# A state-space mixer block: two kernels' filters loaded by channel and turned on TensorE, with step one and the modulation loads reordered

## The chip, the core and the metric

The kernel runs on one core of a Trainium2 chip. The core has a matrix engine (TensorE, in the profile PE, with its weight loads as PEld), three elementwise engines (VectorE or DVE, ScalarE or ACT, GpSimd or POOL), a queue engine that only issues transfers (SyncE or SP), and 16 DMA engines that move data between the chip's memory and the on-chip memory SBUF. TensorE writes its results to PSUM, of which this kernel uses four tiles of 128 x 1024 numbers. Each engine works through its own list of instructions in order; semaphores hold an instruction until what it needs has been done on another engine. The metric is the device time of one execution in microseconds (us).

## The reference

All tensors are float32; S = 2048 tokens, D = 640 channels, F = 1728. Cut to what matters:

```python
mod = (silu(c) @ w_mod).reshape(1, 6, 1, -1);  sa, ca, ga, sb, cb, gb = mod[:, 0], ..., mod[:, 5]
h  = layernorm(x) * (1 + ca) + sa                     # x is A_q
k_shift[t] = sum_s A_k[t - s] * shift_k[:, s]         # causal, 4 taps, per channel
kv = k_shift * A_v
y  = irfft(rfft(kv, 2S) * rfft(ssm_k, 2S))[:S] + kv * ssm_D     # long causal convolution, per channel
x  = x + ga * (h * y)
h  = layernorm(x) * (1 + cb) + sb
x  = x + gb * (gelu(h^T w1 + b1) w2 + b2)^T           # a two-layer network over the token axis
```

The term `kv * ssm_D` is the same as adding `ssm_D` to the first tap of the filter `ssm_k`, and the kernel does that.

## The kernel before, in words

The convolution part goes over five chunks (`c` = 0 to 4) of 128 channels, each in two halves of 64; the network over the tokens follows. A token's number is written as 32 n1 + n2. A partition of SBUF then holds one (half, n1) and, along its free axis, the 32 values of n2 for 64 channels. The transform is done in four small matrix products:

- `step1(side, t)`: step one, over n1. `step1(0, t)` takes kv, which lies in tile X; `step1(1, t)` takes the filter, which lies in tile P under the name KSP. Four calls (t = 0 to 3) make one side. Each is 16 products of a 128 x 64 stationary piece with a 128 x 128 table F1; ScalarE then copies the PSUM tile to Z. KSP's pieces are contiguous, X's have a stride of 32 numbers.
- `f2(g)`, g = 0 to 7: step two, over n2, for both sides, by two tables W2. ScalarE copies the filter's half of the PSUM tile to KT (L249), VectorE multiplies it with kv's half (two products to P, "p<-pst,kt"), and GpSimd adds and subtracts these to the spectrum Y ("y<-p", two a group). P has two buffers for it, so P is both the filter's tile and the products'.
- `i2(r)`, twice: first inverse step, Y to T2. `i1(half)`, twice: second inverse step, by the table V1. `gate` multiplies the result with A1 on VectorE and adds it to x on GpSimd.

PSUM tiles are taken in turn from a ring of three; a fourth, `tap`, holds the taps and the short convolution's sums, and in chunk 0 the modulation's sums.

`kv_ops(g)` is the short convolution of a quarter of a chunk: seven elementwise steps and a product with v that writes a quarter of X. Quarter 2 runs on GpSimd, the others on VectorE. For chunk c + 1 these steps are the list `fill`, from which `dv(n)` takes some between the groups of f2.

The filter of a chunk comes by `load_ks`: two transfers of 64 x 64 pieces of 32 numbers, already in the (half, n1) layout, into KSR (half of the tile `aux`), with `ssm_D` for one partition of each half. `perm_add` adds `ssm_D`, and `perm` on ScalarE (L175) reorders the whole to KSP.

Chunk 0 carries one-time work. `lay_w2(i, n)` on ScalarE (L109) spreads W2 from `xb`, where x's second half will lie. `load_q` brings q (32 transfers, L514) and four of five row blocks of `w_mod` (L346); the fifth goes to P. 16 pairs of `bn_stats` with a `bn_aggr` each (L560, L561), then `rstd`, give the layer norm's scale. `mod_part` (L353) multiplies w_mod's blocks with silu(c), `mod_sum` copies the sums (L357), `mod_row` (L364, copies L371 and L373) spreads three rows over all partitions. `ac` (L300, 16 steps on ScalarE) normalises x into A1, and `po` on VectorE scales and shifts A1 by the modulation, in chunk 0 by halves. w_mod's blocks lie in the tile of V1, and in `aux`, where KSR and A1 also lie; so V1's table (L578) is loaded after `mod_part(1)`, the filter of chunk 1 after `mod_part(2)`.

The order of all of it is written by hand in the program; there is no planner. Transfers carry one of eight semaphores in turn, and each waits on its semaphore's earlier transfer, so the SP queue can stand behind slow transfers. In the list of chunk 0 after f2, the order on TensorE is: four `step1(0, t)` of chunk 1, the transpose of the biases, `i2(0)`, `mod_part` 0 to 3, `i2(1)`, `mod_part` 4, `mod_row`, `i1(0)`, `i1(1)`, four `step1(1, t)`. On ScalarE it is: copies of step one, copies of `i2(0)`, the root, `ac[0:4]`, copies of `i2(1)`, `mod_sum`, `ac[4:8]`, `mod_row`'s copies, `perm(1)`, `ac[8:16]`, copies of step one.

## Time and profile before

| | us |
|---|---|
| median of three runs | 705.45 (703.06 to 716.54) |
| the profiled execution | 705.09 |
| its span in the profile | 703.0 |
| TensorE busy, all matrix products | 643.0 |
| VectorE busy | 494.3 |
| ScalarE busy | 307.9 |
| GpSimd busy | 155.7 |
| first matrix product begins | 23.65 |
| chunk 0's step two (f2) begins | 42.35 |
| chunk 1's step two begins | 113.41 |
| chunk 2's step two begins | 164.86 |
| chunk 3's step two begins | 214.76 |

The span is the time from the first to the last instruction; 2.1 us of the device time lie around it. From one f2 to the next take 71.06 us in chunk 0, where the one-time work lies, and 51.45 and 49.90 us in chunks 1 and 2. A row of the timeline has a start, a length, the engine and line, what is written and read, the shape and the count, and in brackets how long the engine was idle before and what released it. "SPq" and "ACTq" rows are the issuing of transfers, not the transfers themselves.

### The profile page before, as it was taken

To read this page: it belongs to the slowest core of one execution; us is meant where nothing else is said; L and a number is where in the kernel's file an instruction comes from. 1 tells how busy PE (TensorE), PEld (TensorE's weight loads), DVE (VectorE), ACT (ScalarE), POOL (GpSimd) and SP (SyncE) were. 2 spreads that over 40 slices of the span, in tenths; PEclk is the share of its full clock that TensorE was granted. 3 is DMA by queue.
4 is the path that set the end of the run, shared out by engine and by line. 5 is a ranking of instruction groups with operands and counts; after the bars stand their busy time and mean duration, and the time that the engine had idled before them with its cause. 6 is when DMAs were issued, how large, how long until landed. Compare 5 with 4: busy or idle time off the path is not lost.

```text
span 703.0 us, 20726 instructions
## 1 busy us (share of the span) xinstructions
PE 643.0 (91%) x9099; PEld 623.8 (89%) x9099; DVE 494.3 (70%) x865; ACT 307.9 (44%) x477; POOL 155.7 (22%) x135
## 2 busy tenths in 40 slices
PE   0699868989999999987899999999999999999997
PEld 0699558989999999777899999999999999999997
DVE  6678568969879837888895411421398969888886
ACT  0564653635645645645766422422334222333331
POOL 5297038714725527300000000000000000000000
PEclk9999978999999999989889999999999999999999
DMA  9977968527142523352113650353173343555511
GB/s 182 212 221 230 350 135 180 116 48 173 40 86 73 177 54 88 115 133 49 34 28 63 118 104 17 61 115 66 53 195 106 105 137 100 160 171 171 154 55 38
DMA packets 166672, 82.80 MB, mean 118 GB/s; under 512 B 89235, under 2 KB 157622, under 8 KB 166582
## 3 DMA queue, kind: packets, MB, share of 16 engines
q1 hardware_dynamic: 162034, 80.17, 46.2%
q10 hardware_dynamic: 4548, 1.31, 1.1%
q8 instruction: 71, 1.16, 0.7%
q14 instruction: 19, 0.16, 0.1%
HBM read 70.97 MB, written 10.49 MB: 116 GB/s over the span
## 4 chain that ended last, share of the span: by engine, by line
PE 69%; DVE 14%; DMA 6%; POOL 4%; ACT 3%; issue 3%; SPq 1%; ACTq 0%; DVEq 0%; POOLq 0%
PE pst L445 20%; PE pst L1033 18%; PE pst L229 8%; PE pst L1110 7%; PE pst L245 6%; PE pst L274 4%; POOL y L60 4%; PE pst L930 3%; DVE tap L60 2%; DMA aux<-in_A_ssm_k_dram 2%; PE pst L293 2%; DVE kt L60 2%; DMA aux<-in_w_mod_dram 2%; DVE aux L60 2%; DVE p L60 1%
## 5 line engine op out<-in xcount | busy, mean ns | idle before, releaser
L245 PEld LDWEIGHTS pst<-z,w 128*64 128x64 f32 x2560 | 94.7, 141 | 7.7 <-ACT z L231 7.3
L245 PE MATMUL pst<-z,w 128*64 128x64 f32 x2560 | 95.7, 240 | 6.3 <-ACT z L231 6.1
L60 POOL TENSOR_TENSOR y<-p 128x256 f32<-128x256 f32 x72 | 91.9, 1324 | 25.7 <-DVE p L60 25.2
L60 DVE TENSOR_TENSOR p<-pst,kt 128x512 f32<-128x512 f32 x80 | 52.3, 690 | 23.8 <-ACT kt L249 16.1
L229 PE MATMUL pst<-v,x 128*64 128x128 f32 x640 | 45.5, 302 | 23.6 <-DVE x L60 23.6
L231 ACT ACTIVATE z<-pst 128x1024 f32<-128x1024 f32 x40 | 45.6, 1144 | 46.2 <-PE pst L229 26.6
L229 PEld LDWEIGHTS pst<-v,x 128*64 128x64 f32 x640 | 43.6, 221 | 24.1 <-POOL t L470 23.6
L249 ACT ACTIVATE kt<-pst 128x512 f32<-128x512 f32 x40 | 25.2, 631 | 48.0 <-PE pst L245 26.3
L229 PE MATMUL pst<-v,p 128*64 128x128 f32 x640 | 39.9, 285 | 6.5 <-DVE aux L60 5.0
L229 PEld LDWEIGHTS pst<-v,p 128*64 128x64 f32 x640 | 37.4, 144 | 7.8 <-DVE aux L60 5.2
L274 PEld LDWEIGHTS pst<-v,y 32*128 32x128 f32 x1280 | 38.2, 187 | 5.4 <-POOL y L60 2.4
L274 PE MATMUL pst<-v,y 32*128 32x64 f32 x1280 | 40.1, 272 | 2.4 <-DVE y L60 1.4
L1033 PE MATMUL pst<-r_z,m_w 128*128 128x320 f32 x222 | 41.6, 309 | 0.7 <-DVE m_w L60 0.7
L1021 ACT ACTIVATE m_w<-m_v 128x896 fp32r<-128x896 f32 x24 | 22.2, 948 | 38.8 <-DVE m_v L60 23.1
L60 DVE TENSOR_TENSOR tap<-tap,kt 128x512 f32<-128x512 f32 x51 | 35.6, 698 | 1.3
L60 DVE TENSOR_TENSOR kt<-in,tap 128x512 f32<-128x512 f32 x51 | 35.1, 688 | 1.5
L1033 PEld LDWEIGHTS pst<-r_z,m_w 128*128 128x128 f32 x222 | 34.8, 188 | 0.9 <-DVE m_w L60 0.9
L850 ACT ACTIVATE pst<-pst,sm 128x640 f32<-128x640 f32 x14 | 10.7, 766 | 56.0 <-PE pst L445 56.0
L60 DVE TENSOR_TENSOR m_w<-m_v,m_w 128x896 fp32r<-128x896 f32 x24 | 26.0, 1088 | 9.8 <-ACT m_w L1021 9.8
L282 ACT ACTIVATE z<-pst 128x512 f32<-128x512 f32 x38 | 21.5, 666 | 21.1 <-PE pst L274 21.1
L1021 ACT ACTIVATE m_w<-m_p 128x896 fp32r<-128x896 f32 x12 | 11.4, 954 | 41.2 <-DVE m_p L60 24.4
L293 PEld LDWEIGHTS pst<-z,v 64*64 64x64 f32 x1280 | 22.4, 144 | 7.6 <-issue 4.9
(304 smaller groups left out, 1449.5 us busy)
## 6 DMA issues: line engine op xcount, KB each, us to landing
x<-in_B_w_dram SPq DMA_DIRECT2D x20, 512.0 KB
m_v<-in_B_w_dram SPq DMA_DIRECT2D x15, 384.0 KB
x<-in_B_w_dram SPq DMA_DIRECT2D x14, 384.0 KB
aux<-in_A_ssm_k_dram SPq DMA_DIRECT2D x10, 512.0 KB
in<-in_A_k_dram SPq DMA_DIRECT2D x36, 128.0 KB
in<-in_A_v_dram SPq DMA_DIRECT2D x36, 128.0 KB
m_x<-xs SPq DMA_DIRECT2D x28, 160.0 KB
out_dram<-m_x SPq DMA_DIRECT2D x28, 160.0 KB
```

Of the source, the lines that this page charges most:

```text
L60: TT = lambda eng, o, a, b, op: eng.tensor_tensor(o, a, b, op=op)
L229: pe.matmul(ps[64 * ri:64 * ri + 64, o:o + 128], lhs, F1[:, 128 * ri:128 * ri + 128], start=True, stop=True)
L231: evac = lambda: act.activation(Z[:, side, t].rearrange("p a k e -> p e a k"), ps.rearrange("p (e a k) -> p e a k", a=8, e=2), AF.Copy)
L245: pe.matmul(ps[64 * h:64 * h + 64, o:o + 64], W2[k1 // 32][:, 2 * (k1 % 32) + ri], rhs, start=True, stop=True)
L249: act.activation(kt.rearrange("p (m i) -> p m i", i=32), pv[:, :, 1], AF.Copy)
L274: pe.matmul(pp[qd // 2][:, o:o + 64], Y[p, ri, i:i + 2].rearrange("p i k -> p (i k)"), V2[p, 64 * ri:64 * ri + 64], start=ri == 0, stop=ri ...
L282: act.activation(o, i, AF.Copy)
L293: pe.matmul(ps[64 * b:64 * b + 64, 512 * e + 64 * jj:512 * e + 64 * jj + 64], V1[p, ri, n2], T2[p, :, 32 * ri + n2], start=ri == 0, stop=r ...
L445: pe.matmul(ps[0:m, h, 0:320], w_.bitcast(F32R), r_[:, 320 * h:320 * h + 320].bitcast(F32R), start=first and i == 0, stop=last and i == 2)
L1021: act.activation(W[n][0].bitcast(F32R), A[p, w_], AF.Copy)
L1033: pe.matmul(bank[n], w[:, i].bitcast(F32R), r.bitcast(F32R), start=i == 0 and k == 0, stop=i == 6 and k == 2)
L1110: pe.matmul(acc[s][:, h, 0:320], w[:, f_].bitcast(F32R), u[r + h].bitcast(F32R), start=f_ == 0 and k == 0, stop=f_ == NF - 1 and k == 2)
```

## The change

Five edits, all in the work of the first two chunks.

1. The filters of chunks 0 and 1 are loaded by channel: `load_kc` is one transfer with a channel's 2048 taps per partition (128 x 2 x 4096 bytes), and `ssm_D` goes to one number per partition. A 128 x 128 identity, EYE, is loaded beside the small constants.
2. `turn` takes the place of `perm_add` and `perm` for these two chunks. It adds `ssm_D` to one column (ScalarE in chunk 0, GpSimd in chunk 1), makes 64 products of a 128 x 64 stationary piece (stride 32 numbers) with 64 columns of EYE, in two PSUM tiles, and copies each to KSP on ScalarE.
3. In chunk 0 the filter's step one comes ahead of kv's. `lay_w2(0, ...)` stays with kv's step one. The short convolution's quarter 1 of chunk 1 moves from before f2 to `fill`, which now has 16 steps instead of 8.
4. `load_q` is cut in four: eight transfers of q, then one block of w_mod, four times. The first two parts are issued ahead of kv's step one, the last two after `lay_w2(1, 3)` as before.
5. Chunk 0 after f2: the transpose of the biases and the silu move into f2 (at g = 5); `mod_part` 0 to 3 come ahead of `i2(0)`; `ac[0:8]` ahead of the copies of `i2(1)`; `ac[8:16]` and all of `po` ahead of `turn(1)`; GpSimd's quarter 2 of chunk 2 after `turn(1)`'s addition, and all of it ahead of `i1`.

```diff
+    def load_kc(c, eng=sync):
+        sync.dma_start(KSR, dram(ssm_k, DC * c * S, [[S, 128], [1, S]]), max_dma_last_dim=4096)
+        eng.dma_start(dcol[:, c:c + 1], dram(ssm_D, DC * c, [[1, 128], [1, 1]]))
+
+    def turn(c, eng=act):
+        r, d = KSR[:, 0:1], dcol[:, c:c + 1]
+        if eng is act:
+            act.activation(r, r, AF.Identity, bias=d)
+        else:
+            TT(eng, r, r, d, ALU.add)
+        for s in range(2):
+            ps = psum()
+            for n in range(16):
+                for h in range(2):
+                    pe.matmul(ps[64 * h:64 * h + 64, 64 * n:64 * n + 64],
+                              KSR.rearrange("p (a n) -> p n a", n=32)[:, 16 * s + n], EYE[:, 64 * h:64 * h + 64],
+                              start=True, stop=True)
+            act.activation(KSP.rearrange("p i (n e) -> p n e i", e=2)[:, 16 * s:16 * s + 16],
+                           ps.rearrange("p (n e i) -> p n e i", n=16, e=2), AF.Copy)
...
     sync.dma_start(SM, dram(c_small, 0, [[550, 128], [1, 422]]))
-    load_ks(0, act)
+    sync.dma_start(EYE, dram(c_small, 422, [[550, 128], [1, 128]]))
+    load_kc(0, act)
...
-    perm_add(0)
-    perm(0)
+    turn(0)
+    for t in range(4):
+        step1(1, t)
     all_taps()
     load_taps(2)
...
+    load_q(0, 4, 0)
+    load_q(4, 8, 1)
+    lay_w2(0, 0)
     for t in range(4):
         step1(0, t)
-        lay_w2(0, t)
+        if t < 3:
+            lay_w2(0, t + 1)
     run(kv_ops(2, pool))
     run(kv_ops(0))
-    run(kv_ops(1))
-    for t in range(4):
-        step1(1, t)
...
-    fill = kv_ops(3)
+    fill = kv_ops(1) + kv_ops(3)
...
                 if g == 3:
-                    load_q()
+                    load_q(8, 12, 2)
+                    load_q(12, 16, 3)
+            if c == 0 and g == 5:
+                ps = psum()
+                pe.transpose(ps[:, 0:36], stg, ID[0:36, 0:36])
+                act.activation(cols, ps[:, 0:36], AF.Copy)
+                act.activation(sil, cols[:, 30:35], AF.Silu)
...
             for t in range(4):
                 step1(0, t)
-            ps = psum()
-            pe.transpose(ps[:, 0:36], stg, ID[0:36, 0:36])
-            act.activation(cols, ps[:, 0:36], AF.Copy)
-            act.activation(sil, cols[:, 30:35], AF.Silu)
-            i2(0)
             for kk in range(4):
                 mod_part(tap, kk, pl[kk])
...
                 if kk == 2:
-                    load_ks(1)
+                    load_kc(1)
+            i2(0)
             rstd(rs1, nm1, 0, 16)
-            run(ac[0:4])
-            i2(1)
+            run(ac[0:8])
             mod_part(tap, 4, pl[4])
...
+            i2(1)
             mod_sum(tap, T_kt[:, 0:640])
-            run(ac[4:8])
             pool.tensor_scalar(PW, TR.rearrange("p (i s) -> p s i", s=4), 1.0, None, op0=ALU.mult)
-            run(kv_ops(2, pool))
             for i in range(3):
                 mod_row(i, T_kt[:, 0:640])
+            run(ac[8:16])
+            run(po)
+            turn(1, pool)
+            run(kv_ops(2, pool))
             taps()
             load_taps(3)
-            perm_add(1, dve)
-            perm(1)
             load_ks(2)
-            run(ac[8:16])
-            run(po[0:2])
```

More of the change, by code (lines that the diff above doesn't have):

```diff
@@ L42, in _constants @@
     v1 = np.tile(np.stack([np.cos(ang), np.sin(ang)], 1).reshape(64, 4096) / 2048, (2, 1))
-    sel = np.zeros((128, 128))
-    sel[0, 0:64] = sel[1, 64:128] = 1
-    small = np.concatenate([f1.reshape(128, 256), v2, np.eye(128)[:, 0:36], np.tile(np.eye(2), (64, 1)), sel], 1)
+    small = np.concatenate([f1.reshape(128, 256), v2, np.eye(128)[:, 0:36], np.tile(np.eye(2), (64, 1)),
+                            np.eye(128)], 1)
     return {"small": small.astype(np.float32), "w2": w2.reshape(128, 4096).astype(np.float32),
@@ L132, in mixer_kernel @@
     epsc = small(1)
+    dcol = small(2)
     B1C, B2C = cols[:, 0:14], cols[:, 14:30]
@@ L659, in mixer_kernel @@
                 k0 = step1(1, 0, True)
-            elif half:
-                run(po[2:4])
             gate(c, ps, half)
```

17 lines of the change are left out of this document (8 added, 9 removed).

## The prediction, made before the changed kernel ran

> **What bounds the kernel now.** I read the page's chain of waits first, then the same chain in order of time. Only chunks 0 and 1 are changed, so only the chain up to chunk 1's step two matters. Columns: start, length, what the chain goes through.
>
> ```profile
> 1.94 3.96 DMA in<-in_A_k_dram
> ...
> 42.35 19.09 PE pst L245 x505
> ...
> 65.82 10.93 DMA aux<-in_w_mod_dram
> ...
> 78.82 15.99 DMA aux<-in_A_ssm_k_dram
> ...
> 106.11 6.13 PE pst L229 x64
> ...
> 112.26 1.10 ACT z L231
> ...
> 113.41 2.61 PE pst L245 x63
> ```
>
> TensorE sets the end, except where a load does. There are two such places: 23.65 us before the first product, and the stretch from the end of f2 to 113.41, where the chain runs through w_mod (10.93) and then through chunk 1's filter (15.99). While that filter is late, ScalarE's list stands at `perm`, with `ac[8:16]`, `po` and the gates queued behind. I call T0 the start of chunk 0's f2 (42.35) and T1 that of chunk 1's (113.41); T1 - T0 is 71.06. All the change can do is move T0 and T1 - T0. After T1 nothing is altered, and I count it at nothing: chunk 2's filter is asked for earlier, not later.
>
> **T0.** The early part, first all engines, then TensorE alone, then ScalarE alone:
>
> ```profile
> 9.95 0.36 SPq L465 DMA_DIRECT2D v<-in_const_small_dram  x1
> ...
> 11.22 5.05 SPq L163 DMA_DIRECT2D aux<-in_A_ssm_k_dram  x2
> ...
> 21.27 1.28 ACT L175 ACT_TABLE_LOAD   x1 [21.27 <-DMA aux<-in_A_ssm_k_dram]
> ...
> 40.21 11.04 SPq L514 DMA_DIRECT2D xa<-in_A_q_dram  x16
> ```
>
> ```profile
> 23.65 10.52 PE L229 MATMUL pst<-v,x 128*64 128x128 f32 x128 [23.65 <-DVE x L60]
> 33.98 7.17 PE L229 MATMUL pst<-v,p 128*64 128x128 f32 x128
> 42.35 19.00 PE L245 MATMUL pst<-z,w 128*64 128x64 f32 x511 [1.20 <-ACT z L231]
> ...
> 61.25 8.24 PE L229 MATMUL pst<-v,x 128*64 128x128 f32 x127
> ```
>
> ```profile
> 33.26 1.15 ACT L109 ACTIVATE w<-xb,v 128x1024 f32<-128x1024 f32 x1
> 34.30 1.16 ACT L231 ACTIVATE z<-pst 128x1024 f32<-128x1024 f32 x1
> ```
>
> And TensorE by stage (busy time, records, granted clock as noted, DMA share, GB/s):
>
> ```profile
> 24.00:27.00 3.00, 3.00 (x32) 1.00 1.29 191
> 36.00:39.00 3.00, 3.00 (x60) 1.00 0.93 338
> 80.00:83.00 3.00, 3.00 (x98) 1.00 1.02 410
> ```
>
> The old filter was there at 21.27, 5.0 after its last issue ended (16.27). In the new order it is third after the small constants, behind EYE; at the 1.27 from 9.95 to 11.22 a place, it is issued at 12.5. A transfer of 128 KB took 3.96 from issue to landing (the chain's first row above); the other 0.9 MB at the rate of the 4096-byte rows of V1's table (410 GB/s in the last stage) adds 2.2. So it lands at 18.7; bounds 16.6 (1 MB alone after 1.5) and 21.3 (as before).
>
> A profile record is half a product here: step one has 16 products and 32 records. `turn` has 64 products, so 128 records. No row has its shape. Its stationary piece is X's (128 x 64, stride of 32 numbers), with half the streamed columns. X's step one takes 8.24 / 128 = 64 ns a record, KSP's contiguous one 7.17 / 128 = 56; f2, with 64 columns and contiguous pieces, 19.0 / 511 = 37. If streaming is the limit, `turn` takes 128 x 37 = 4.8; if the strided weight load is, 8.2; at the mean of X's first, slow pass (10.52 / 128 = 82) 10.5. I take 8.2: with equal streaming only the stride can explain X's 64 against KSP's 56.
>
> The sum: landed 18.7, addition on ScalarE 0.3 (an estimate), turn 8.2, last copy 1.15 (as L231's, of equal size), the filter's step one 7.2, kv's 8.2, last copy 1.15: 44.9, which is 2.5 later than 42.35. What is gained is the wait to 23.65 and the slow start that X's pass paid: 32 records in 3 us at first, 60 later (the clock column says 1.00 there only because nothing is on record so early). Now `turn` stands in that slow time. ScalarE doesn't add: a `lay_w2` and a copy start 1.04 apart, 2.08 a group against step one's 2.06.
>
> The Trainium skill ("TensorE: Matmul & The Clock Gate", section LDWEIGHTS) has a weight load take its column count / 1.2 ns whatever the pattern: 53 ns for 64 columns, so 6.8 us a turn and 2.8 less in the end. The trace doesn't settle it: X's 64 ns speaks for more, f2's 37 for less.
>
> **f2 with sixteen fill steps instead of eight.** VectorE in f2 before:
>
> ```profile
> 45.62 1.29 DVE L60 TENSOR_TENSOR p<-pst,kt 128x512 f32<-128x512 f32 x2 [3.45 <-ACT kt L249]
> 46.84 0.68 DVE L60 TENSOR_TENSOR tap<-tap,kt 128x512 f32<-128x512 f32 x1
> 47.55 0.72 DVE L60 TENSOR_TENSOR kt<-in,tap 128x512 f32<-128x512 f32 x1
> 48.16 1.28 DVE L60 TENSOR_TENSOR p<-pst,kt 128x512 f32<-128x512 f32 x2
> ...
> 63.42 0.88 DVE L560 BATCH_NORM_STATS2 sm<-xa 128x6 f32<-128x320 f32 x2
> ```
>
> GpSimd's additions in f2, as a group (count, busy time, mean ns):
>
> ```profile
> L60 POOL TENSOR_TENSOR y<-p 128x256 f32<-128x256 f32 x16 | 20.3, 1329 | 1.2 <-DVE p L60 1.2
> ```
>
> The pair of products takes 1.22 from start to start, a fill step 0.66. The last step of quarter 0 writes X, so now it waits for kv's step one, which ends at T0 - 1.2, and all of quarters 1 and 3 stands behind it on VectorE. Before, X was free at 34.2 (23.65 + 10.52) with the filter's step one still to come, so quarters 0 and 1 were done ahead of f2. From T0: three steps to +1.6, pair 0 at +3.3 (45.62 - 42.35) to +4.5; with 3, 3, 3, 2, 2 steps between, pairs end at 7.8, 11.0, 14.3, 17.0, 19.5. f2(g) needs the PSUM tile of three groups before, and the transpose at g = 5 takes one of the ring, so f2(6) waits for pair 4 (17.0) and f2(7) for pair 5 (19.5). f2 ends at +21.9 instead of 61.25 - 42.35 = +18.9, the last pair at +23.8 instead of +21.1 (63.42). GpSimd, two additions a pair of 1.27 (20.3 / 16), ends at +26.6, hidden by the step one that follows. Cost 3.0 on TensorE, 2.7 on VectorE.
>
> **From f2 to T1.** Durations before:
>
> ```profile
> 70.67 3.79 PE L274 MATMUL pst<-v,y 32*128 32x64 f32 x124 [0.63 <-ACT z L231]
> ...
> 74.31 2.23 ACT L282 ACTIVATE z<-pst 128x512 f32<-128x512 f32 x4 [2.10 <-PE pst L274]
> ...
> 74.38 2.35 PE L353 MATMUL tap<-v,sm 128*32 128x320 f32 x24
> ...
> 76.56 1.28 ACT L337 ACT_TABLE_LOAD   x1
> ...
> 78.13 11.29 SPq L163 DMA_DIRECT2D aux<-in_A_ssm_k_dram  x2
> ...
> 79.59 0.31 ACT L337 ACTIVATE sm<-sm 128x16 f32<-128x16 f32 x1 [1.75 <-DVE sm L561]
> ...
> 81.52 1.65 ACT L300 ACTIVATE aux<-xa,sm 128x128 f32<-128x128 f32 x4 [1.62 <-DVE sm L342]
> ...
> 86.29 0.72 ACT L357 ACTIVATE kt<-tap 96x640 f32<-96x640 f32 x1
> ...
> 87.06 1.37 PE L364 MATMUL pst<-kt,sm 1*128 1x320 f32 x12 [1.61 <-ACT kt L357]
> ...
> 88.44 0.70 ACT L371 ACTIVATE g<-pst 128x640 f32<-128x640 f32 x1
> ...
> 95.19 2.49 DVE L60 TENSOR_TENSOR aux<-aux,g 128x1024 f32<-128x1024 f32 x2
> ...
> 100.47 4.25 DVE L60 TENSOR_TENSOR aux<-aux,g 128x1024 f32<-128x1024 f32 x2 [1.47 <-ACT aux L300]
> ...
> 149.71 2.10 PE L293 MATMUL pst<-z,v 64*64 64x64 f32 x128
> ```
>
> From T0, in the new order: f2 ends 21.9; kv's step one 8.2, 30.1; `mod_part` 0 to 3, 48 records at 2.35 / 24, 4.7, 34.8; `i2(0)` 3.8, 38.6; its copies 2.2 on ScalarE, 40.8; the root's table 1.3, 42.1. The 16 statistics, 63.42 to 79.59 and so 16.1, end at 39.9 and are hidden by 2.2; before they were what the root waited for. Root to first `ac` 1.9 (79.59 to 81.52), 44.0; eight `ac` at 0.41, 47.3; copies of `i2(1)` 2.0, 49.3; `mod_sum` to `mod_row` 0.8 (86.29 to 87.06), 50.1; to the first copy of a row 1.4, 51.5; that copy, which frees `turn`'s PSUM tile, 0.7, 52.2; `turn(1)` 8.2, 60.4; `i1` twice 4.2, 64.6; the filter's step one 4 x 1.85 = 7.4 (the pace of 7.17 with its hand-overs), 72.0; copy 1.1. T1 - T0 = 73.1, against 71.06: 2.0 more.
>
> Beside this path: `ac[8:16]` ends at 56, `po` (a pair of 2.49, and one of 4.25 as where GpSimd worked beside it) by 60.5, so the gates wait for `i1`, not for `po`. w_mod's first four blocks need only be there at T0 + 30: 36 issues of q and w_mod at 0.69 (11.04 / 16) from 36 on (q could start at 40.21 before, and all ahead of it in SP's list comes some 5 sooner) and 10.93 to land end at T0 + 27, so that wait goes. SP is past chunk 1's filter with one issue instead of 11.29 us of it, so k and v of chunk 2 are asked for some 10 us sooner and GpSimd's quarter 2 is done before `po`'s second half. The filter is released by `mod_part(2)` at T0 + 33.6, behind V1's 2 MB: 3 MB at 410 GB/s plus 2 is T0 + 43, 9 before `turn(1)`. Were it later than that, each microsecond over 9 would count in full.
>
> So the 15.99 us wait goes, but the time is taken by what is late next: the modulation's sums, which wait on ScalarE behind the root and eight `ac`, then 8.2 us of products that TensorE didn't have. **Sum: 2.5 + 2.0 = 4.5 on the profiled 705.09 (span 703.0 and 2.1 around it): 709.6.** That execution is 0.4 under the median of the runs shown.
>
> **Rivals.** (a) Streaming sets the pace of the turns: 4.8 us each, the filter at 16.6. That takes off 3.4 twice and 2.1: 700.7. For it: f2's 37 ns at equal columns. Against: X's 64. (b) The identity products don't warm the clock, and the first of the filter's step one runs as the first of kv's did: 10.52 - 8.24 = 2.3, once, at T0: 711.9. The Trainium skill ("TensorE: Matmul & The Clock Gate", Part 4: PE-mode transpose) says that transposes in that mode don't count as busy for the clock. No run here shows it. These are plain products. TensorE also stands still from T0 + 43 to + 50 ahead of `turn(1)`; were both turns at 82 ns, 2.3 each, 714.2. (c) The other side: weight loads of strided pieces no longer hide. Count, busy time and mean ns of X's on the page:
>
> ```profile
> L229 PEld LDWEIGHTS pst<-v,x 128*64 128x64 f32 x640 | 43.6, 221 | 24.1 <-POOL t L470 23.6
> ```
>
> Each takes 221 ns, and they cost 64 only because about three are under way at once. If 64 columns are too short to cover them and each waits for the one before, a turn is 128 x 0.221 = 28.3, 20.1 more twice: 749.8. It decides from about 100 ns a record on (4.8 more a turn), where the kernel is 2% slower. Against it: f2's loads hide behind equally short products. (d) The change doesn't do what it says: the filter's transfer, behind V1, is late again and `turn(1)` waits at T0 + 60 instead of 52: 8 more, 717.6.
>
> **Chances.** Forecast (706 to 713) 0.46; (a) and the stretch from it to 705, 0.25; (b) 0.15; (d) 0.05; (c) or another pile-up beyond 719 0.06; a gain of over 14 us 0.03. A measurement of this kernel tells about 2% (14 us) from no change. The range 700 to 717 takes in the bounds of landing and turn, and leaves out (c), (d) and what lies under (a). Faster by over 2% 0.03, slower 0.07, the rest within.
>
> **What would show it.** The first identity product at 18 to 19 us, 128 records in about 8 us each time, f2 of chunk 0 from 44.9 and lasting 22, no wait of TensorE for w_mod or the filter, the root's table directly ahead of the root with the statistics done before it, chunk 1's f2 at about 118. It is wrong if a turn takes 5 us, or if f2 isn't stretched by VectorE, or if TensorE still waits for a load between f2 and T1.

## The result, and the profile after

The changed kernel takes 712.96 us (median of four runs, 711.82 to 714.70). Beside the kernel before it is 1.011 times as long, with a 95% interval of 1.0072 to 1.0147: slower by 1.1%, less than the 2% that the prediction took for the limit of what can be told apart, and yet clearly told apart. Two of the runs of the kernel before (716.54 and 716.56) were in a slower state, which some executions of any kernel are in, and the ratio leaves them out. The profiled execution took 711.82 us, its span 710.0, against 705.09 and 703.0 before: 7.0 more of span.

TensorE's work in order of time, in the changed kernel, up to the start of chunk 1's f2 (start, length, what, in brackets the idle time before it and what ended it):

```profile
19.29 8.09 PE L194 MATMUL pst<-rows,aux 128*64 128x64 f32 x128 [19.29 <-ACT aux L187]
29.38 8.61 PE L250 MATMUL pst<-v,p 128*64 128x128 f32 x128 [2.00 <-ACT p L197]
37.83 8.16 PE L250 MATMUL pst<-v,x 128*64 128x128 f32 x128
47.53 14.65 PE L266 MATMUL pst<-z,w 128*64 128x64 f32 x384 [1.55 <-ACT z L252]
...
64.62 5.07 PE L266 MATMUL pst<-z,w 128*64 128x64 f32 x128 [2.26 <-DVE p L59]
69.48 8.29 PE L250 MATMUL pst<-v,x 128*64 128x128 f32 x128
...
97.15 2.53 PE L385 MATMUL pst<-kt,sm 1*128 1x320 f32 x12 [4.14 <-ACT kt L378]
100.49 8.13 PE L194 MATMUL pst<-rows,aux 128*64 128x64 f32 x128 [0.81 <-POOL t L59]
108.55 4.17 PE L314 MATMUL pst<-z,v 64*64 64x64 f32 x256
112.65 0.88 PE L250 MATMUL pst<-v,p 128*64 128x128 f32 x12
114.48 6.55 PE L250 MATMUL pst<-v,p 128*64 128x128 f32 x116 [0.95 <-issue]
122.20 3.03 PE L266 MATMUL pst<-z,w 128*64 128x64 f32 x76 [1.17 <-ACT z L252]
```

T0 is 47.53 (before 42.35, so 5.2 later) and T1 122.20 (before 113.41, 8.8 later); T1 - T0 has grown from 71.06 to 74.67. The two waits of TensorE for loads are gone: no row between 69.48 and 122.20 is released by a DMA. In their place stand the turn (8.13), and a wait of 4.14 for the modulation's sums on ScalarE. The chain of waits, in order of time, goes another way through the same stretch (start, length, what it goes through):

```profile
94.74 2.50 POOL t L59 x2
...
100.49 8.13 PE pst L194 x128
```

It leads through GpSimd's work on quarter 2, because that work's fourth step happened to end at 99.92. The turn has no need of it: its addition to the filter stands ahead of it in GpSimd's list, and ended at 93.1. What it waited for is its PSUM tile, freed by the copy of the first modulation row, which starts at 99.69 and takes 0.70. The releaser in a chain is inferred, and has to be held against the list of the program.

The same stretch by windows of TensorE (busy time, records, granted clock, DMA share, GB/s):

```profile
30.00:31.00 1.00, 1.00 (x14) 0.50 0.97 219
...
33.00:34.00 1.00, 1.00 (x22) 1.00 0.96 381
...
95.00:97.00 2.00, 0.00 (x0) 0.50 0.54 124
...
101.50:102.50 1.00, 1.00 (x22) 0.50 0.88 202
...
104.50:106.00 1.50, 1.50 (x29) 1.00 0.00 0
```

A window counts every record that it touches, so that the counts are a little above the pace. Behind chunk 0's turn the clock falls to 0.50 (28.90 to 32.31), and 14 records of step one touch a microsecond instead of 22. It falls once more at 90.34 and is back at 103.99, so the rows ran at half clock: 2.53 instead of 1.37. ScalarE's row of the turn's second copy:

```profile
27.41 1.91 ACT L197 ACTIVATE p<-pst 128x1024 f32<-128x1024 f32 x1 [1.81 <-PE pst L194]
```

It takes 1.91, where L231's of the same 128 x 1024 numbers took 1.16 in the kernel before. After T1 1.8 comes back: chunk 1, from its f2 to chunk 2's, takes 50.26 (122.20 to 172.46) instead of 51.45, and the rest 0.6 less.

### The profile page after: what moved, and what is told of

It is laid out like the page before. It is cut to its first block, busy times and chain, and to the rows that moved or that the text cites. A ratio compares the mean times of both kernels' runs of the same rounds, so it can differ in the third digit from the quotient of the medians.

```text
span 710.0 us, 21234 instructions
## 1 busy us (share of the span) xinstructions
PE 651.9 (92%) x9355; PEld 632.9 (89%) x9355; DVE 494.2 (70%) x863; ACT 312.6 (44%) x480; POOL 153.9 (22%) x134
## 4 chain that ended last, share of the span: by engine, by line
PE 62%; DVE 16%; DMA 6%; POOL 6%; ACT 4%; issue 3%; SPq 3%; ACTq 0%; DVEq 0%; POOLq 0%
PE pst L466 17%; PE pst L1054 17%; PE pst L1131 7%; PE pst L250 5%; PE pst L295 4%; POOL y L59 4%; PE pst L266 4%; PE pst L951 3%; DVE tap L59 2%; DMA in<-in_A_k_dram 2%; PE pst L314 2%; DVE p L59 2%; DVE kt L59 2%; DMA xa<-in_A_q_dram 1%; SPq L143 1%
## 5 line engine op out<-in xcount | busy, mean ns | idle before, releaser
L250 PE MATMUL pst<-v,x 128*64 128x128 f32 x640 | 43.1, 292 | 0.0
L250 PEld LDWEIGHTS pst<-v,x 128*64 128x64 f32 x640 | 41.4, 220 | 0.5
L250 PE MATMUL pst<-v,p 128*64 128x128 f32 x640 | 38.3, 280 | 3.4 <-ACT p L197 2.0
L250 PEld LDWEIGHTS pst<-v,p 128*64 128x64 f32 x640 | 36.4, 141 | 4.1 <-ACT p L197 2.1
L1042 ACT ACTIVATE m_w<-m_v 128x896 fp32r<-128x896 f32 x24 | 22.2, 948 | 38.0 <-DVE m_v L59 23.8
L194 PEld LDWEIGHTS pst<-rows,aux 128*64 128x64 f32 x256 | 16.0, 220 | 21.0 <-ACT aux L187 19.3
L194 PE MATMUL pst<-rows,aux 128*64 128x64 f32 x256 | 16.2, 312 | 20.1 <-ACT aux L187 19.3
```

Source lines behind the costliest of these rows:

```text
L194: pe.matmul(ps[64 * h:64 * h + 64, 64 * n:64 * n + 64], KSR.rearrange("p (a n) -> p n a", n=32)[:, 16 * s + n], EYE[:, 64 * h:64 * h + 64] ...
L250: pe.matmul(ps[64 * ri:64 * ri + 64, o:o + 128], lhs, F1[:, 128 * ri:128 * ri + 128], start=True, stop=True)
L1042: act.activation(W[n][0].bitcast(F32R), A[p, w_], AF.Copy)
```

## The experiments

In what follows, T1 - T0 and the length of a chunk are differences of the starts of f2 in TensorE's rows. Ratios are to the kernel before, with 95% intervals; a single run has none.

**A second profile of both kernels, first, since it says how far one profile can be trusted.** Nothing is edited.

> The changed kernel once more, unaltered, for a second profile. If T0 (47.5), the clock's fall behind the turn and f2's length (22.1, no stop marked issue) belong to the kernel, they are the same within 0.3; if they belong to the execution, T0 is 46.0 as in the kernels with the same head and no fall (46.0 and, with shorter turns, 43.4), or f2 is 24 to 25.

> The kernel before once more, unaltered, for a second profile. If f2 without stops (19.1) belongs to the kernel, it is 19.1 again, and T0 42.3; if stops come with the execution, f2 is 20 to 22 in some executions of it too, and T0 41.0 to 42.4 as in the kernels that share its head.

TensorE's rows of the changed kernel, second execution, and then of the kernel before, second execution:

```profile
29.34 8.87 PE L250 MATMUL pst<-v,p 128*64 128x128 f32 x128 [2.00 <-ACT p L197]
...
47.71 14.48 PE L266 MATMUL pst<-z,w 128*64 128x64 f32 x384 [1.43 <-ACT z L252]
```

```profile
42.04 18.98 PE L245 MATMUL pst<-z,w 128*64 128x64 f32 x511 [1.18 <-ACT z L231]
```

T0 is 47.71 and 42.04, f2 22.2 and 19.0, T1 - T0 74.91 and 71.13: all within 0.3 of the first. The slow step one behind the turn came again. Only some places where the clock falls differ from one execution to the next: in the kernel before 90.56 and 104.21 in the first, 72.69, 89.75 and 106.82 in the second. The differences belong to the kernels, as far as two executions of each can say.

**The head undone.** Chunk 0 as before; chunk 1's turn and w_mod among q's loads stay.

```diff
-    load_kc(0, act)
+    load_ks(0, act)
...
-    turn(0)
-    for t in range(4):
-        step1(1, t)
+    perm_add(0)
+    perm(0)
...
+    run(kv_ops(1))
+    for t in range(4):
+        step1(1, t)
-    fill = kv_ops(1) + kv_ops(3)
+    fill = kv_ops(3)
```

> Chunk 0 as in the kernel before (its filter by partitions and copied, kv's step one first, quarter 1 of kv ahead of f2); chunk 1 by channels and turned, w_mod among q's loads. Theory: the loss lies in chunk 0's head. Then T0 is 42.4 as before (47.53 in the changed kernel), f2 lasts 18.9 (22.1), and the rest of T1 - T0 is as in the changed kernel: T1 - T0 = 74.67 - 3.2 = 71.5, some 8 us off 712: 704, the same as before within 0.5%. Rival: the turn of chunk 1 and its hand-overs cost most of it: then T0 + f2 come back but T1 - T0 stays near 74, and the time is 707 to 709. Second rival: q starts later here (40 instead of 37), so w_mod is late at T0 + 27 and TensorE waits for it, up to 6 us: 705 to 710.

715.49 us, ratio 1.0104 (1.0055 to 1.0152). T0 came back as expected, to 41.46, but T1 - T0 rose to 85.4. TensorE's rows, then its windows:

```profile
80.78 2.36 PE L374 MATMUL tap<-aux,sm 128*32 128x320 f32 x12 [6.82 <-DMA aux<-in_w_mod_dram]
83.07 7.11 PE L295 MATMUL pst<-v,y 32*128 32x64 f32 x128
```

```profile
88.00:90.00 2.00, 2.00 (x44) 0.50 1.25 235
```

The second rival holds in kind: w_mod is late by 6.8. Its total of 705 to 710 is passed all the same, because the clock falls in that wait (at 78.49), so that `i2(0)` takes 7.11 instead of 3.80, and because f2 lasts 20.7. With the old head SP asks for q at 41.72, with the new one at 36.96: w_mod among q's loads is there in time only behind the new head.

**Chunk 1's turn undone.**

```diff
-                    load_kc(1)
+                    load_ks(1)
...
-            turn(1, pool)
+            perm_add(1)
+            perm(1)
```

> The changed kernel with chunk 1's filter loaded by partitions and copied on ScalarE, in the place of the turn. TensorE has 8.1 us less to do between the rows of the modulation and the inverse step. Theory 1: the turn stands on the path with its whole 8.1 us: T1 - T0 falls from 74.7 to about 66.5, 704. Theory 2: the products of VectorE with the modulation's rows (7.4 us, until T0 + 62) and the gates behind them take the turn's place, since the inverse step's two PSUM tiles wait for the gates: T1 - T0 about 70.5, 708. Rival: the filter, 11.3 us of issues behind V1, lands at T0 + 50 or later and TensorE waits for it: T1 - T0 74 or more, 712 and above. T0 stays at 47.5 in all.

711.24 us, ratio 1.0078 (1.0042 to 1.0114). From f2's end to T1 the changed kernel needs 52.5 (69.7 to 122.2) and this one 48.0:

```profile
69.64 1.64 PE L266 MATMUL pst<-z,w 128*64 128x64 f32 x40 [0.96 <-issue]
...
112.66 5.46 PE L250 MATMUL pst<-v,p 128*64 128x128 f32 x96 [1.23 <-DVE aux L59]
119.31 19.57 PE L266 MATMUL pst<-z,w 128*64 128x64 f32 x512 [1.19 <-ACT z L252]
```

Of the turn's 8.1 us 4.5 come back, and VectorE's products and the gates (its `aux`, until 113.7) take the place of the rest: theory 2. T1 - T0 is 73.3 and not its 70.5, because f2 lasted 25.2 here, with stops of 4.3 marked issue. T0 was 46.0 here, not 47.5: with the same pause behind the turn the clock did not fall.

**The copy behind the turn.**

```diff
-            act.activation(KSP.rearrange("p i (n e) -> p n e i", e=2)[:, 16 * s:16 * s + 16],
-                           ps.rearrange("p (n e i) -> p n e i", n=16, e=2), AF.Copy)
+            act.activation(KSP.rearrange("p i (n e) -> p i n e", e=2)[:, :, 16 * s:16 * s + 16],
+                           ps.rearrange("p (n e i) -> p i n e", n=16, e=2), AF.Copy)
```

> Only the copy behind a turn is altered: it runs through its output in order (32 numbers in a row) and reads PSUM with a stride, where the changed kernel reads in order and writes with a stride of 256 bytes. Theory: the stride of the writes makes the copy 2.0 us instead of 1.15. Then the copies take 1.15 to 1.3, the filter's step one begins 0.8 earlier and T0 is 46.7 or, if the shorter pause also spares the clock's fall to 0.50, 45.3; 710 to 712. Rival: the strided read costs as much, or more: copies of 2 us, T0 47.5, no change.

ScalarE's row, then TensorE's:

```profile
27.17 1.02 ACT L197 ACTIVATE p<-pst 128x1024 f32<-128x1024 f32 x1 [2.86 <-PE pst L194]
```

```profile
28.24 7.21 PE L250 MATMUL pst<-v,p 128*64 128x128 f32 x128 [1.12 <-ACT p L197]
...
44.90 13.12 PE L266 MATMUL pst<-z,w 128*64 128x64 f32 x348 [1.31 <-ACT z L252]
60.36 2.09 PE L266 MATMUL pst<-z,w 128*64 128x64 f32 x36 [2.33 <-issue]
```

With the stride on the side of the reads a copy is shorter by 0.9. The pause is 1.12, the clock stays up (7.21) and T0 is 44.90, a little under the 45.3 that was expected if the clock is spared. The kernel gained nothing by it in this one run, 713.38: f2 took 24.2, with a stop of 2.33, marked issue, after 348 records, 28 into its sixth group and so not at a tile's hand-over; the profile names no cause.

**The pause filled with identity products.**

```diff
     turn(0)
+    ps = psum()
+    for n in range(8):
+        for h in range(2):
+            pe.matmul(ps[64 * h:64 * h + 64, 64 * n:64 * n + 64],
+                      KSR.rearrange("p (a n) -> p n a", n=32)[:, 16 + n], EYE[:, 64 * h:64 * h + 64],
+                      start=True, stop=True)
```

> 16 more identity products (32 records, 2.05 us), whose result nobody reads, fill the pause of TensorE between chunk 0's turn and the filter's step one. Theory: identity products hold the clock, and the pause of 2.0 us lets it fall to 0.50 for 3.4 us. Then the clock stays at 1.00 and the first group of step one takes 1.8 instead of 3.4: T0 46.1 instead of 47.5, 710 to 712. Rival: identity products don't count for the clock, which is low for that reason: the first group takes 3.4 again, with a clock of 0.50, and T0 is 47.6.

TensorE's rows:

```profile
27.42 2.16 PE L520 MATMUL pst<-rows,aux 128*64 128x64 f32 x32
29.74 7.21 PE L250 MATMUL pst<-v,p 128*64 128x128 f32 x128 [0.17 <-ACT p L197]
```

Step one runs at full pace at once, so identity products hold the clock. That it was the pause that let it fall is likely, not shown by this one run: the same pause, unfilled, also passed without a fall in two other kernels. T0 is 46.44; one run of 714.42 shows no gain in the whole.

**kv's step one first.**

```diff
     turn(0)
-    for t in range(4):
-        step1(1, t)
...
+    run(kv_ops(1))
+    for t in range(4):
+        step1(1, t)
-    fill = kv_ops(1) + kv_ops(3)
+    fill = kv_ops(3)
```

> The changed kernel with kv's step one back ahead of the filter's in chunk 0, and quarter 1 of kv ahead of f2. The turn's last copy is then beside kv's step one, and X is free about 10 us sooner. Theory: the order of the two step ones costs both the pause behind the turn (2.0, and 1.4 of slow clock) and the longer f2. Then T0 is 19.2 + 8.1 + 8.2 + 7.2 + 1.2 = 44.0 instead of 47.5, f2 lasts 19 to 20.5 instead of 22.1, and it ends near 64 instead of 69.7; w_mod's last two blocks, which land near 75 to 80, are then waited for by 2 to 5 us, and the time is 707 to 710. Rival: f2 still lasts 22, because something else than quarter 1 stretches it: 709 to 712.

712.94 us, ratio 1.0093 (1.0051 to 1.0134). TensorE's rows:

```profile
43.57 8.46 PE L266 MATMUL pst<-z,w 128*64 128x64 f32 x222 [1.19 <-ACT z L252]
54.96 4.71 PE L266 MATMUL pst<-z,w 128*64 128x64 f32 x127 [2.92 <-issue]
61.96 1.50 PE L266 MATMUL pst<-z,w 128*64 128x64 f32 x35 [2.30 <-issue]
```

T0 is 43.57, as worked out. f2 lasts 24.9, but 5.2 of it are two stops with no cause named, after 222 and 349 records; the 2.26 of waiting for VectorE is gone. So quarter 1 did stretch f2, and the stops stretched it here. TensorE did not wait for w_mod, as had been expected. The expected total was missed by 3.

**Whole weight loads.**

```diff
-                              KSR.rearrange("p (a n) -> p n a", n=32)[:, 16 * s + n], EYE[:, 64 * h:64 * h + 64],
+                              KSR.rearrange("p (n a) -> p n a", n=32)[:, 16 * s + n], EYE[:, 64 * h:64 * h + 64],
```

> Both turns read their stationary pieces as 64 neighbouring numbers instead of 64 numbers at a stride of 128 bytes: as many products, of equal size, but the filter's values come out in another order, so this kernel leaves out the regrouping of the filter. Theory: the strided weight load sets the turn's 64 ns a record; without it 37 (f2's pace) to 56 (the pace of the filter's step one), a turn 4.8 to 7.2 instead of 8.1. Rival: the products themselves take 64 ns: 8.1 again, 712. A second point: the copy behind the turn is not altered and should still take 2.0.

TensorE's rows, the two turns, and two windows of the second with their clock:

```profile
19.01 5.65 PE L194 MATMUL pst<-rows,aux 128*64 128x64 f32 x128 [19.01 <-ACT aux L187]
...
97.16 5.81 PE L194 MATMUL pst<-rows,aux 128*64 128x64 f32 x128 [0.81 <-POOL t L59]
```

```profile
99.00:101.00 2.00, 2.00 (x43) 0.50 0.21 44
101.00:103.00 2.00, 2.00 (x66) 0.93 0.00 0
```

44 ns a record (5.65 / 128) against 63 (8.09 / 128): the stride costs 2.4 us a turn. But the 44 is a mean of two paces. By the starts of its records the second turn makes one every 53 ns as long as the clock is at 0.50 (to 101.29) and one every 29 ns behind that; the first turn has the same two paces, changing at 22.8, where no clock is on record. With the stride, in the changed kernel, a record starts every 61 ns at 0.50 and every 62 at 1.00. So the stride sets a pace that the clock doesn't touch, and costs 8 ns a record at half clock and 32 at full clock; a turn without it, all at full clock, is 3.7 us by these numbers (128 x 29 ns, an estimate). The one run took 708.66, 4.3 under the changed kernel's median.

**w_mod ahead of q, on the kernel before.** Its own filters and order, but w_mod's blocks first, the sums ahead of `i2(0)`, and the transpose of the biases in f2 as in the changed kernel.

```diff
     perm(0)
+    for kk in range(4):
+        mod_load(0, kk, (T_v1[:, 0:1920], T_v1[:, 1920:3840], T_aux[:, 0:1920], T_aux[:, 2048:3968])[kk])
...
-            i2(0)
             for kk in range(4):
                 mod_part(tap, kk, pl[kk])
...
+            i2(0)
             rstd(rs1, nm1, 0, 16)
```

> The kernel before, with its own filter loads, but w_mod's first four blocks asked for ahead of q, and the modulation's products for them ahead of i2(0). It takes away only the wait for w_mod. Theory: the wait of 10.93 in the chain is worth what TensorE stood for it (1.2 us) and what the filter, released by the third block's products, gains: these begin at 69.5 instead of 74.4, so the filter is asked for 5 us sooner (73 instead of 78.1) and T1 comes 4 to 5 us sooner, 700. Rival: the gates, which waited for VectorE until 106 in the kernel before, don't move, and the filter's step one behind them neither: T1 112 to 113, 704 to 706, no change.

704.06 us, ratio 0.9984 (0.9941 to 1.0026): no change. T0 is 40.98 and T1 108.30, 5.1 sooner than before as expected; then chunk 1 takes 54.59 instead of 51.45. SP's row, GpSimd's, TensorE's, and a window of TensorE:

```profile
73.60 13.01 SPq L163 DMA_DIRECT2D aux<-in_A_ssm_k_dram  x2
```

```profile
96.01 2.54 POOL L60 TENSOR_TENSOR t<-in,t 128x512 f32<-128x512 f32 x2 [13.43 <-DMA in<-in_A_k_dram]
```

```profile
108.30 14.38 PE L245 MATMUL pst<-z,w 128*64 128x64 f32 x384 [1.19 <-ACT z L231]
...
132.92 5.46 PE L274 MATMUL pst<-v,y 32*128 32x64 f32 x128 [0.75 <-DVE y L60]
```

```profile
137.00:137.85 0.85, 0.85 (x23) 0.50 0.00 0
```

The filter's issues hold SP for 13 us, k of chunk 2 waits behind them, and GpSimd stands 13.4 for it. It begins 2.9 sooner than in the kernel before (98.93), but T1 is 5.1 sooner: its gate additions run 5.2 into chunk 1 instead of 2.6, a pause of 0.75 follows ahead of `i2`, the clock is at 0.50 from 135.41 on and `i2` takes 5.46. So taking the wait for w_mod away, 10.93 in the chain, brings T1 5.1 sooner, gives 3.1 back in chunk 1, and leaves nothing that this measurement can tell from no change. This kernel is the base of the next ones, since w_mod is never late in it.

**One part of the change at a time on that base.** First chunk 1's turn, then the head:

```diff
-                    load_ks(1)
+                    load_kc(1)
...
-            perm_add(1, dve)
-            perm(1)
+            turn(1, dve)
```

> The kernel with w_mod ahead of q (704.06; T1 - T0 67.3; chunk 1 54.6), with one part of the change added: chunk 1's filter by channels and turned on TensorE in the place of the copy. This prices the turn of chunk 1 with w_mod never late. Theory 1: the turn takes 8.1 us of TensorE ahead of i1, of which 4 to 5 show at T1, since the gates waited for VectorE until 103 anyway; SP is past the filter with one issue instead of 13 us of them, so GpSimd's quarter 2 and its gate additions come sooner and chunk 1 takes 50.3 again instead of 54.6: in sum 703 to 706, no change. Theory 2: all 8.1 us are on the path and nothing is given back: 709 to 713.

```diff
-    load_ks(0, act)
+    load_kc(0, act)
...
-    perm_add(0)
-    perm(0)
+    turn(0)
+    for t in range(4):
+        step1(1, t)
...
-    fill = kv_ops(3)
+    fill = kv_ops(1) + kv_ops(3)
```

> The kernel with w_mod ahead of q (704.06), with the other part of the change added: chunk 0's filter by channels and turned, its step one ahead of kv's, and so quarter 1 of kv in f2. This prices the head with w_mod never late. Theory: T0 goes from 41.0 to 42.4 up to 46.0 to 47.5 and f2 from 19.5 to 22.2, together 7 us later at the end of f2, and as TensorE is the bound from there to T1 nearly all of it stays: 709 to 712. Rival: the later start gives waits behind f2 time to go (modulation rows, gates), and 3 or more come back: 704 to 708.

The turn alone: 709.72 us, ratio 1.0073 (1.0050 to 1.0096), 5.7 over the base. The head alone: 714.55, ratio 1.0139 (1.0097 to 1.0180), 10.5 over it. The changed kernel has both, with w_mod among q and another order of `ac`, `po` and `i2(1)`; it is 8.9 over the base, so the prices don't add. With the turn alone, TensorE's row and VectorE's:

```profile
97.28 8.15 PE L194 MATMUL pst<-rows,aux 128*64 128x64 f32 x128 [3.52 <-issue]
```

```profile
95.98 1.20 DVE L59 TENSOR_TENSOR aux<-aux,sm 128x1 f32<-128x1 f32 x1
```

T1 is 119.89, 11.6 later than the base's 108.30. 2.5 of that are there at the end of f2 (63.50 instead of 60.97), 2.3 for stops marked issue. The other 9.1 are the 8.15 of the turn and 3.52 in which it waits, less what other waits give up. Nothing is named for the 3.52, but VectorE's addition to the filter, queued behind the rows' products there, ends at 97.18, just ahead of the turn. 4.4 come back in chunk 1 (50.16 instead of 54.59), 3.3 of them ahead of its `i1`: GpSimd is done with the gates at 117.46, ahead of T1. That SP is free sooner is not shown to be the reason, since the later T1 alone would do for it. With the head alone, TensorE's rows:

```profile
117.04 3.71 PE L250 MATMUL pst<-v,p 128*64 128x128 f32 x64 [3.79 <-DVE aux L59]
121.93 19.59 PE L266 MATMUL pst<-z,w 128*64 128x64 f32 x512 [1.18 <-ACT z L252]
```

T0 is 47.31 and T1 121.93, and it is the gates that end the last wait. Either part alone brings T1 to 120 to 122, and so do both: what one adds, the other's waits hide.

**Where the turn stands.** Three edits of order. In the changed kernel, the rows ahead of the scalings; on the base with the turn, the rows and the turn ahead of `i2(1)`; on the base, three pauses filled:

```diff
             i2(0)
-            rstd(rs1, nm1, 0, 16)
-            run(ac[0:8])
             mod_part(tap, 4, pl[4])
+            rstd(rs1, nm1, 0, 16)
+            mod_sum(tap, T_kt[:, 0:640])
+            for i in range(3):
+                mod_row(i, T_kt[:, 0:640])
+            run(ac[0:8])
...
             i2(1)
-            mod_sum(tap, T_kt[:, 0:640])
...
-            for i in range(3):
-                mod_row(i, T_kt[:, 0:640])
```

> The changed kernel with the modulation's sums and rows straight behind the root, ahead of the row scalings (ac) and of i2(1), instead of behind them. Theory: the rows, which in the changed kernel waited on ScalarE until 97.2 with TensorE standing still for 4.1 us, then start near 91; VectorE's products with them and the gates come 4 us sooner, the turn begins at 97 instead of 100.5, and T1 - T0 is 70 to 71 instead of 74.7: 707 to 709. Rival: i2(1) now waits for the rows' PSUM tiles, and the turn behind it begins no sooner: T1 - T0 74, 712.

713.39 us, ratio 1.0123 (1.0093 to 1.0154), T1 - T0 75.4: the rival.

```profile
90.46 1.97 PE L385 MATMUL pst<-kt,sm 1*128 1x320 f32 x12 [3.26 <-ACT kt L378]
93.16 7.69 PE L295 MATMUL pst<-v,y 32*128 32x64 f32 x128 [0.73 <-ACT g L392]
```

The rows come 6.7 sooner and `i2(1)` moves behind them, at half clock (7.69); the turn begins where it did, at 100.77.

```diff
...
-                if kk == 1:
-                    sync.dma_start(T_v1[:, 0:4096], c_v1, max_dma_last_dim=4096)
                 if kk == 2:
                     load_kc(1)
+                    sync.dma_start(T_v1[:, 0:4096], c_v1, max_dma_last_dim=4096)
             i2(0)
+            mod_part(tap, 4, pl[4])
             rstd(rs1, nm1, 0, 16)
+            mod_sum(tap, T_kt[:, 0:640])
+            for i in range(3):
+                mod_row(i, T_kt[:, 0:640])
             run(ac[0:4])
+            turn(1, pool)
             i2(1)
-            mod_part(tap, 4, pl[4])
...
-            mod_sum(tap, T_kt[:, 0:640])
...
-            turn(1, dve)
```

> The kernel with w_mod ahead of q and chunk 1's filter turned (709.7), with the filter asked for ahead of V1's table, the last block's sums and the rows straight behind i2(0), the turn between the rows and i2(1), and the turn's copies writing in order. Theory: what the turn cost was its place: here it fills a stretch in which TensorE stood still or waited, at a pace (64 ns) that the fallen clock doesn't slow. From the rows at about 83 the turn ends near 92, i2(1) 96, i1 101, the filter's step one 109: T1 108 to 110, chunk 1 50.2 as in the kernel with the turn, chunk 2 from 159 instead of 164.9, 698 to 701. Rival: TensorE has no free time between f2 and T1, its 8.1 us are paid wherever they stand: T1 115 to 120, 706 to 710.

712.28 us, ratio 1.0097 (1.0055 to 1.0139), T1 117.70: the rival again, with a total 2 above its own.

```profile
87.52 8.18 PE L194 MATMUL pst<-rows,aux 128*64 128x64 f32 x128 [0.81 <-issue]
...
101.65 5.59 PE L314 MATMUL pst<-z,v 64*64 64x64 f32 x256 [2.23 <-ACT z L303]
```

The turn ends at 95.6 (92 was expected) and `i2(1)` runs at full pace behind it, in 3.80. But nothing is left for TensorE to do while ScalarE copies `i2(1)` (2.14, from 99.46), and the inverse step begins at 101.65. No place of 8 us was free here either.

```diff
             i2(0)
+            for _ in range(10):
+                pe.matmul(tap[96:128, 896:1024], F1[:, 0:32], F1[:, 0:128], start=True, stop=True)
...
```

> The kernel with w_mod ahead of q, with 10, 8 and 7 products that nobody reads (128 x 32 by 128 x 128, about 0.1 us each) in three pauses of TensorE of 0.8 to 1.0 us: behind i2(0), behind the last block's sums, and ahead of chunk 1's i2(0). In the kernel without them the clock fell to 0.50 at 80.6 for 13.7 us and at 135.5 for 6.8 us. Theory: these pauses make the clock fall, and with them filled it stays at 1.00: the rows come 3 to 4 us sooner, T1 - T0 is 63 to 65 instead of 67.3, and chunk 1 loses 3 less: 697 to 701. Rival 1: the clock falls all the same, because i2 (32 rows of 128) doesn't hold it, or products on a fourth of the columns don't: 704 to 706. Rival 2: the clock stays, but the gates and GpSimd's late work set the end: 702 to 704.

715.60 us, ratio 1.0169 (1.0118 to 1.0219). None of the theories: the third filling had to wait itself.

```profile
90.19 1.37 PE L364 MATMUL pst<-kt,sm 1*128 1x320 f32 x12 [0.85 <-ACT kt L357]
...
140.89 3.17 PE L636 MATMUL tap<-v 128*32 128x128 f32 x14 [5.45 <-DVE tap L60]
```

With the first two the clock stayed up to 92.11 (rows 1.37 instead of 2.53), but the rows did not come forward (90.19 against 87.94 in the base). The third writes into `tap`, which VectorE still used for kv. The total therefore says nothing of the clock's price.

**A new order from f2 to T1.** The sums behind f2, the filter's step one ahead of `i1`:

```diff
...
+            for t in range(4):
+                run(ac[4 * t:4 * t + 4])
+                step1(1, t)
...
-        for t in range(1 if c else 0, 4):
+        for t in range(1 if c else 4, 4):
             step1(1, t)
```

> As the last one, and the order from f2 to T1 is changed: the modulation's products come straight behind f2, then kv's step one, the last block's products, i2(0), the rows, i2(1), the filter's step one with the sixteen row scalings (ac) between its groups, and i1 and the gates at the end. The filter (by partitions, copied) is asked for at T0 + 23. TensorE's own work from T0 to T1 adds up to f2 18.9, sums 5.9, kv's step one 8.2, i2 7.6, rows 1.4, the filter's step one 7.2, i1 4.2: 53.4. ScalarE, from the statistics' end at T0 + 37.2, has root and table 1.6, copies 2.2, filter copy 1.3, ac 6.6, copies of step one 4.6: T0 + 53.5. Theory: the order sets T1 - T0 and no load does: T1 - T0 about 56 instead of 71.06, 690 to 693. Rival: VectorE's products with the rows and the gates behind them hold two of three PSUM tiles into chunk 1's f2, and 3 to 6 us of it are given back there: 694 to 698. Second rival: the filter's 16 us from issue to landing end past T0 + 42 and TensorE waits: 698 and above.

716.89 us, ratio 1.0137 (1.0052 to 1.0222), T1 - T0 78.9 instead of 56. In this order the filter's step one overwrites the numbers that `i1` reads, so that `i1` here works on others of equal count.

```profile
79.56 1.45 PE L353 MATMUL tap<-p,sm 128*32 128x320 f32 x12 [3.43 <-DMA p<-in_w_mod_dram]
80.94 7.11 PE L274 MATMUL pst<-v,y 32*128 32x64 f32 x128
...
103.39 9.36 PE L229 MATMUL pst<-v,p 128*64 128x128 f32 x128 [3.76 <-ACT p L175]
```

TensorE waits 3.43 for w_mod's last block, and from 80.53 on the clock is at 0.50 for 27.3 us: `i2(0)` takes 7.11 instead of 3.80, and `i2(1)` 7.1. ScalarE copies `i2(1)` at 99.28 and only then the filter, for which step one waits 3.76. Which of these waits weighs most, no run here takes apart.

## Why the prediction was right or wrong, step by step

- **The sign and most of the sum held; the size was too small.** 4.5 us were forecast, the profiled execution shows 6.7 (711.82 against 705.09). T0 is 5.2 later instead of 2.5, T1 - T0 3.6 longer instead of 2.0, and 1.8 come back where nothing was counted. The mechanism of both stretches was right; what failed is the size of T0's sum, and with it the claim of the next point.
- **"A measurement of this kernel tells about 2% from no change" failed.** Four runs were enough to put 1.1% outside its own interval. The 0.07 for slower and 0.9 for the rest stand on that limit, which did not hold. The sum itself, 709.6, is 1.006 of the profiled 705.09 and so was the forecast of a slower kernel.
- **Filter and turn: right.** ScalarE's addition began at 18.94, the turn took 8.09 and 8.13 against 8.2. The reason was right as well: without the stride the records come faster, one every 29 ns at full clock, under the 37 of rival (a). So rival (a)'s pace is there for contiguous pieces, and the stride is what kept the turn from it. The slow start that kv's step one had paid cost the turn nothing, since its pace is the same at both clocks. The Trainium skill ("TensorE: Matmul & The Clock Gate", section LDWEIGHTS) works a weight load out from its column count alone, 53 ns for 64 columns. That is the pace here without the stride at a clock of 0.50; at 1.00 it is 29, and with the stride 61 to 62 at both, so pattern and clock count as well. Rival (c) fell: each load takes 220 ns in the turn too, at 63 a record, so they overlap.
- **The failed step of T0: "last copy 1.15 (as L231's, of equal size)".** Equal size, but not equal layout: it writes at a stride of 256 bytes and took 1.91, a pause of 2.00 on TensorE instead of 1.15. Behind that pause the second term failed, the filter's step one: 8.45 from its start to the next instead of 7.2. These two are 2.1 of the 2.6 that T0 came later than 44.9; 0.4 more is the last copy, which waited on ScalarE for a `lay_w2` ("ScalarE doesn't add"), and 0.3 the filter's landing. With the stride on the reads the copy took 1.02, step one 7.21, and T0 was 44.90.
- **Step one at half clock: rival (b) in effect but not in cause.** The filter's step one ran at a clock of 0.50 from 28.90 to 32.31. Not because identity products don't warm the clock: chunk 1's turn raised it from 0.50 to 1.00 at 103.99 with nothing beside it on TensorE but its own products, and where the clock did not fall, step one ran at full pace (7.21) straight behind the turn. The fall came behind the pause of 2.0 in four profiles (both of the changed kernel, the head alone, the rows ahead of the scalings), not in two others with the same pause (chunk 1's turn undone, whole weight loads), and not where the pause was filled or 1.12 long, in one run each. So the pause is needed, as far as these runs go, and not always enough. The Trainium skill (the same page, Part 4: PE-mode transpose) says that transposes in that mode do not count as busy. No run here tests that mode; the turn's plain products do count. That rival (b)'s 711.9 lies beside the profiled 711.82 is luck: it had 2.3 for the clock, and neither the longer copy nor the 1.8 that came back.
- **f2 stretched by VectorE: right.** f2 ended at T0 + 22.1 (forecast 21.9), the statistics began at + 24.1 (23.8), the wait of 2.26 stands where it was put, before the seventh group.
- **From f2 to T1: the places right, two sizes off.** Rows at + 49.6 (forecast 50.1), the turn at + 53.0 (52.2), no wait for w_mod or the filter. But the rows took 2.53 at half clock instead of 1.37, and the filter's step one 8.4 with a stop of 0.95 (no cause shown) instead of 7.4. These two make the 1.6 that T1 - T0 is over its sum of 73.1; the turn begins 0.8 late, and step one takes 1.0 longer.
- **"After T1 I count it at nothing": 1.8 off.** Chunk 1 is 1.2 shorter, but not because SP is past the filter sooner: up to `i1` it takes 36.3 before and 36.4 after, and behind that the kernel before has two stops marked issue (0.70 and 1.34), the changed one a single stop of 0.99. What comes back there is a difference of stops, and so as open as they are.
- **What stays open.** TensorE's stops marked issue, together 0 to 5.2 us in chunk 0's f2: no run shows what they wait for (the last section says where they stand), and part of the differences between the experiments is theirs. No version beat the kernel before: the best, w_mod ahead of q, is level with it.

## What to carry to other kernels

A wait in a chain is not worth its length: here 10.93 and 15.99 us, where TensorE stood for 1.2 and, behind the filter's copy and the gates, 5.5. Taking the first away brought T1 5.1 sooner, and the whole kernel nothing that could be told. Before a load's layout is turned into products, look whether the bounding engine has free time where they must stand, and count what the pauses around them do to its clock. Price a copy by a row of equal layout, not of equal size.

## What was not expected of the hardware

- ScalarE's copy of 128 x 1024 numbers from PSUM: 1.9 to 2.2 us with writes at a stride of 256 bytes, 1.02 to 1.03 with reads at a stride and writes in runs of 32 numbers.
- Products with 64-column stationary pieces of float32: at a column stride of 128 bytes a record starts every 61 to 62 ns, at a clock of 0.50 and of 1.00 alike; with neighbouring columns every 53 ns at 0.50 and every 29 at 1.00.
- The clock falls to 0.50 after pauses of 2.0 us and less, in some executions and at some places only. The Trainium skill ("TensorE: Matmul & The Clock Gate", Part 1: The HAM clock gate) has it fall after an idle window of about 3.4 us; the runs show that less is enough. The shortest pauses before a fall are 0.63 (the kernel before, second execution, 72.69) and 0.75 us, both with `i2` behind them. `i2`'s products on 32 rows did not bring the clock back in 7.1 us without a pause (83.1 to 90.2 in the kernel with the head undone), where the turn's identity products on 128 rows did within 2.7 to 5.7 us of its start.
- In every run the falls and returns of the clock lie on steps of 3.41 us: in the changed kernel it is low for 3.41 us from 28.90 and for 13.65 us from 90.34. In the kernel with chunk 1's turn undone such a step (28.48) cuts the pause behind the first turn into 1.2 and 0.8 us, and the clock stays. That this is why is not shown: with whole weight loads 1.5 us of the pause lie between two steps, as in the changed kernel, and it stays too.
- TensorE's stops marked issue come at the same counts: 222 or 349 records into chunk 0's f2 in most of the experiments (after 222, 349 or both), whatever runs beside it, with lengths of 0.2 to 3.2 us. Counted from the first product of the program they stand at 478, 605, 732 and 857 records, and later, in other runs or the same, at 1239, 1367, 1494, 1621, 1749, 2641 and 2769 (the kernel before has those at 1367, 2641 and 2769): about 127 records apart, or a multiple of that. So they hang on a place in TensorE's own list of instructions; why is open.
